# A convolution and two expert layers in one program: copy order in a bank's release, a shared bank for mixed halves, and a re-planned head

## The chip, the core and the metric

The kernel runs on one core of one Trainium2 chip. The core has five engines that run side by side, each through its own list of instructions in a fixed order: TensorE (PE) multiplies matrices into the eight PSUM banks, VectorE (DVE), ScalarE (ACT) and GpSimd (POOL) work elementwise, and SyncE (SP) issues DMAs. GpSimd has no access to PSUM here; everything it reads and writes is in SBUF. An engine whose next instruction waits for a semaphore holds up all that stands behind it. The metric is the device time of one execution, the median of several; smaller is better.

## The reference

Three layers follow each other on 2 batches of 4160 tokens with 192 features, all in float32 (the weights arrive as 64-bit floats and are narrowed on the chip):

```python
# 1: a causal convolution of 7 taps, weights per token and head
w = softmax(weight_gen)                       # 8 heads x 7 taps
out = einsum('bshk,bskhg->bshg', w, x_unf)    # x_unf: 7 shifted copies of x
# 2: a mix with the token before, then a gated expert
xk = mu_k * x + (1 - mu_k) * x_prev;  xr = mu_r * x + (1 - mu_r) * x_prev
v = relu(xk @ w_k) ** 2 @ w_v;  x = sigmoid(xr @ w_r) * v        # d_ff = 1024
# 3: a second expert with a convolution of 3 taps over tokens
h = relu(x @ w_in);  c = sum_k conv_w[k] * h[shifted by k - 1]
out = (h * sigmoid(c)) @ w_out
```

## The kernel before

The sequence is cut into ten tiles of 256, 248, seven times 472, and 352 tokens. Features lie on partitions, tokens on columns. Each float32 product is made of a high and a low part (fp32r), so one chunk of 128 hidden units costs five matmuls going in and five coming out.

For each tile, GpSimd computes layer 1 token group by token group (`attention`): one multiplication of a 128x1344 piece by the softmax weights, two folding additions, one addition into `tok`. TensorE transposes `tok` into a bank of the pair `pa` (`mixing`, `flip`), ScalarE and VectorE make the two mixed halves (k = 0 for `xk`, k = 1 for `xr`), which are split into high (`hi`) and low (`lo`) parts; for the 64 remaining features four DMAs place them in `xB`. There are three such mixings per tile, u = 0, 2, 1. In the first tile the two mixed halves stood in the PSUM banks `am` and `ar`, which later hold the accumulated sums of `moe1`.

`moe1` runs eight chunks fi per batch: matmuls into `pa`, relu, square and a rounded copy on ScalarE, the remainder on VectorE, five matmuls into `am` (128 rows) and `ar` (64 rows and a shared 64-row part). `mix_out` empties the two banks after each batch: VectorE multiplies them by the gates (d1 for `ar`, d0 for `am`), ScalarE copies the rounded high parts into `x2` (a1 from `ar`, in two copies of 128 and 64 rows; a0 from `am`), VectorE writes the low parts (d3 from `ar`, d2 from `am`). Until these are done the next batch's first sums cannot be written. `moe2` is layer 3: eight chunks through the banks `pc`, summed in `bm` and `br`.

In the head, before and while the first tile runs, the weights are narrowed (`prepare`, `narrow`: one ScalarE instruction, then five on VectorE, through the banks `bm`, `br`, `pc`), split, and the softmax weights are computed (`softmax`: reduction, subtraction, exp, reduction, reciprocal, multiplication). ScalarE holds one function table at a time; going from Sigmoid to Exp or back is an ACT_TABLE_LOAD.

The order of each engine's list is written by a planner, `Program.schedule`. Every operation has a due time (`at(t, ...)`) and an assumed duration (`cost`); the planner plays the engines forward, takes on each engine the ready operation with the earliest due time, and emits the instructions in the order of their planned starts. So a changed assumed duration or due time moves instructions on all engines. In it a PSUM bank is one region whatever part is touched. `cost` took a VectorE reduction to go at 960 elements per microsecond, and it looked at the tensors other than the output when it asked whether a source lies in PSUM; for an in-place operation that list was empty.

Of the kernel before, what the change touches and what calls it, by code (L numbers as in the profile page):

```python
# [35 lines left out]
class Program:  # L36
# [37 lines left out]
    def cost(self, eng, method, out, ins, pointer):  # L74

        n = self.count(out)
        src = [self.space(x) for x in ins]
        if method == "dma_start":
            return 0.6, 0.0
        if eng == "PE":  # L80
            busy = max(n * 0.00045 + 0.002, 0.109)
            return busy, busy + 0.24
        if eng == "ACT":
            near = bool(src) and src[0] == "PSUM"
            p = 0.1 if pointer else 0.0
            return (0.06 if near else 0.09) + p + n / 1200, (0.2 if near else 0.24) + p + n / 1200
        if eng == "DVE":
            if method == "tensor_reduce":
                n = self.count(ins[0])
            if method == "reciprocal":  # L90
                return 0.07 + n / 160, 0.2 + n / 160
            if method in ("tensor_scalar", "tensor_copy", "memset") and "PSUM" not in src:
                return 0.07 + n / 1920, 0.2 + n / 1920
            stt = method == "scalar_tensor_tensor"
            return (0.13 if stt else 0.07) + n / 960, (0.26 if stt else 0.2) + n / 960
        if eng == "POOL":
            busy = 0.1 + (n / 455 if method == "tensor_tensor" else n / 270)
            return busy, busy + 0.12
        return 0.6, 0.6

    def schedule(self):
        n = len(self.ops)
        succ, left, ready, dur, late, moved = [[] for _ in range(n)], [0] * n, [0.0] * n, [0.0] * n, [0.0] * n, [0.0] * n
        shares = [False] * n
        log = {}
        for i, (eng, method, a, k, _, hold) in enumerate(self.ops):
            ready[i] = hold
            aps = [x for x in [*a, *k.values()] if hasattr(x, "tensor") and hasattr(x, "ap")]
            out = k["out"] if "out" in k else aps[0]
            ins = [x for x in aps if x is not out]  # L110
            dur[i], late[i] = self.cost(eng, method, out, ins, any(x is not None and x in ("scale",) and hasattr(k[x], "tensor") for x in k))
            if method == "dma_start":
                moved[i] = self.count(out) * out.ap[0][1] * 4 / 240e3 if self.space(out) != "DRAM" else self.count(ins[0]) * ins[0].ap[0][1] * 4 / 240e3

            src = [self.space(x) for x in ins if self.count(x) > 1]
            shares[i] = eng == "POOL" or eng == "DVE" and (
                src == ["SBUF", "SBUF"] or method in ("tensor_scalar", "tensor_copy") and self.space(out) == "SBUF" and src == ["SBUF"])
            before = set()
            for x, write in [(x, False) for x in ins] + [(out, True)]:
                name, p0, p1, f0, f1 = self.region(x)  # L120
                seen = log.setdefault(name, [])
                keep = []
                for e in seen:
                    j, w, q0, q1, g0, g1 = e
                    if (w or write) and p0 < q1 and q0 < p1 and f0 < g1 and g0 < f1:
                        before.add(j)
                        if write and p0 <= q0 and q1 <= p1 and f0 <= g0 and g1 <= f1 and j != i:
                            continue
                    keep.append(e)
                keep.append((i, write, p0, p1, f0, f1))  # L130
                log[name] = keep
            before.discard(i)
            left[i] = len(before)
            for j in before:
                succ[j].append(i)
        free = dict.fromkeys(self.real, 0.0)
        port, table = 0.0, None
        wires = dict.fromkeys(self.real, 0.0)
        open_ = {e: [] for e in self.real}
        for i in range(n):  # L140
            if not left[i]:
                open_[self.ops[i][0]].append(i)
        start = [0.0] * n
        for _ in range(n):
            t, eng = min((max(free[e], min(ready[i] for i in w)), e) for e, w in open_.items() if w)
            i = min((i for i in open_[eng] if ready[i] <= t), key=lambda i: (self.ops[i][4], i))
            open_[eng].remove(i)
            if shares[i]:
                t = max(t, port)
                port = t + dur[i]  # L150
            turn = 0.0
            if eng == "ACT" and self.ops[i][1] == "activation" and self.ops[i][2][2] in (ACTF.Exp, ACTF.Sigmoid):
                turn = 0.0 if self.ops[i][2][2] == table else 1.3
                table = self.ops[i][2][2]
            start[i] = t
            free[eng] = t = t + turn
            free[eng] += dur[i]
            end = t + late[i]
            if self.ops[i][1] == "dma_start":
                wires[eng] = max(wires[eng], t + dur[i] + 0.6) + moved[i]  # L160
                end = wires[eng] + 0.8
            for j in succ[i]:
                ready[j] = max(ready[j], t + dur[i] if eng == "PE" == self.ops[j][0] else end)
                left[j] -= 1
                if not left[j]:
                    open_[self.ops[j][0]].append(j)
        for i in sorted(range(n), key=lambda i: (start[i], i)):
            eng, method, a, k = self.ops[i][:4]
            getattr(self.real[eng], method)(*a, **k)  # L169
# [14 lines left out]
def conv_moe_kernel(ctx: ExitStack, tc: tile.TileContext, xp, wg_first, wg_rest, mus, w_k, w_v, w_r, w_in, conv_w, w_out, out):  # L184
    nc = tc.nc
    prog = Program(nc)
    PE, ACT, DVE, POOL, SP = (prog.engine(e) for e in ("PE", "ACT", "DVE", "POOL", "SP"))
# [59 lines left out]
    att_r = ring("att", 2, [128, NMAX])  # L247
# [35 lines left out]
    def at(t, fn, hold=0.0):  # L283
        plan.append((t, len(plan), fn, hold))
# [169 lines left out]
    def mixing(i, u, t, dt_):  # L454
        N, P, e = SIZES[i], PART[i], EXTRA[i]
        c = 1 if u == 2 else 0
# [11 lines left out]
        def shifted(fn):  # L468
            a = att_r()[:, :N]
            if e:  # L470
                fn(a, st["q"][:, e - 1:e + N - 1])
            else:
                POOL.memset(a[:, 0:1], 0.0)
                fn(a[:, 1:N], st["q"][:, 0:N - 1])
            return a

# [2 lines left out]
            DVE.tensor_tensor(a, a, st["p"], op=ALU.subtract)  # L479

        def m1(k):
            st[k] = (am_r, ar_r)[k]() if i == 0 else mk_r()
            col = 2 * k + c
            own = slice(col, col + 1)
            if i < 2:
                a = shifted(lambda y, x: ACT.activation(y, x, ACTF.Copy, scale=onemu[:, own]))
                DVE.scalar_tensor_tensor(out=st[k][:, :N], in0=st["p"], scalar=mu[:, own], in1=a, op0=ALU.mult, op1=ALU.add)
            else:
                DVE.scalar_tensor_tensor(out=st[k][:, :N], in0=st["d"], scalar=onemu[:, own],
                                         in1=st["p"], op0=ALU.mult, op1=ALU.add)  # L490
# [120 lines left out]
    def mix_out(i, b, t):  # L611
        N = SIZES[i]
        X = x2[b]
        c = slice(2, N + 2)
        m, r = am_r.tiles[0], ar_r.tiles[0]

        def d0():
            DVE.tensor_tensor(m[:, :N], r_t[0][:, :N], m[:, :N], op=ALU.mult)

        def d1():  # L620
            DVE.tensor_tensor(r[:, :N], r_t[1][:, :N], r[:, :N], op=ALU.mult)

        def a0():
            ACT.copy(X[:, 0, c], m[:, :N])

        def a1():
            ACT.copy(X[:, 2, c], r[:, :N])
            ACT.copy(X[0:64, 3, c], r[0:64, :N])

        def d2():  # L630
            DVE.tensor_tensor(X[:, 1, c], m[:, :N], f(X[:, 0, c]), op=ALU.subtract)

        def d3():
            DVE.tensor_tensor(X[64:128, 3, c], r[0:64, :N], f(X[0:64, 2, c]), op=ALU.subtract)

        at(t, d1)
        at(t + 0.14, d0)
        at(t + 0.15, a1)
        at(t + 0.3, a0)
        at(t + 0.4, d3)  # L640
        at(t + 0.5, d2)
# [94 lines left out]
    def identity():  # L736
        POOL.memset(ident, 0.0)
        POOL.affine_select(out=ident, in_=ident, compare_op=ALU.not_equal, fill=1.0, base=0,
                           pattern=[[-1, 128]], channel_multiplier=1)

    at(-101, identity)
    at(-100.5, consts)
    softmax_load(0, wg_first, -100)
    softmax(0, 0, slots[0], DVE, (-95, -94.9, -94.8, -94.7, -94.6, -94.5), am_r.tiles[0])
    attention(0, 0, -99.9, -90, 0.1, POOL)
    attention(0, 1, -99.6, -83.7, 0.1, POOL)
    softmax_load(1, wg_rest[:, :slots[1] * KH], -99.5)
    softmax(1, 0, slots[1], POOL, (-82.6, -82.5, -82.4, -82.35, -82.3, -82.25), ar_r.tiles[0])
    prepare((-99.75, -99.7, -99.4), [(-82, chunk_rem(w_k, wkB, True)), (-81, chunk_in(w_k, wkA, 0)),
                                     (-0.5, chunk_out(w_v, wv, 0)), (0.4, chunk_out(w_v, wv, 1)), (1.0, chunk_in(w_k, wkA, 1)),  # L750
                                     (1.4, chunk_out(w_v, wv, 2)), (2.4, chunk_out(w_v, wv, 3)), (3.4, chunk_r()),
# [99 lines left out]
```

## Time and profile before

| | us |
|---|---|
| median of 3 runs | 779.31 |
| lowest, highest run | 778.96, 781.27 |
| profiled execution | 780.29 |
| its span from first to last instruction | 778.5 |
| outside the span (780.29 less 778.5) | 1.79 |

Busy times over the whole span are PE 694.1 us (89%), ACT 665.5 us (85%), DVE 630.8 us (81%) and POOL 506.6 us (65%). Such shares average over three unlike stretches: the head up to about 160 us, in which weights are narrowed and the first tiles pass; the long middle; and the drain of the last tile from about 740 us. The profile gives the TensorE clock that was granted, as a share of full speed: its mean over the span is 0.974. A row of a timeline reads: start, duration, engine, line, operation, tensor written, tensors read, count, and in brackets how long the engine sat idle before it and what ended that. Almost all instructions carry L169, the planner's emitting line, so they are told apart by their tensors.

### The profile page before, as it was taken

The page shows a single profiled execution, that of the slowest core. Times are in us where ns is not written, and L with a number is a line of the kernel's source. Part 1 is how long each engine was busy: PE and PEld are TensorE (multiplying, and loading weights), DVE is VectorE, ACT ScalarE, POOL GpSimd, SP SyncE. Part 2 cuts the span into 40 slices and gives each one's busy share as a digit, 9 for nine tenths or more (in the row PEclk, how much of TensorE's full clock was granted, in tenths as well). Part 3 has the DMA queues.
Part 4 walks back from the last instruction along what each step waited for, and adds up shares of the span by engine and source line. Part 5 has one row for each costly group of instructions (what it writes and reads, how often), then busy time and mean ns, then how long its engine had stood idle before and what let it go on. Part 6 is the DMA issues. An engine that isn't in the chain of part 4 may idle for free.

```text
span 778.5 us, 10782 instructions
## 1 busy us (share of the span) xinstructions
PE 694.1 (89%) x3505; PEld 606.3 (78%) x3505; DVE 630.8 (81%) x1137; ACT 665.5 (85%) x1441; POOL 506.6 (65%) x368
## 2 busy tenths in 40 slices
PE   0065776999999999999999999999999999999985
PEld 0054676898888888888888888888888888888974
DVE  6997977886878787878787888788788878788886
ACT  2466797998989898989998989898989899999985
POOL 6998888899999999999999798565702010110000
PEclk9996886999999999999999999999999999999999
DMA  7685010130130112111221120120002000200000
GB/s 224 197 269 180 4 52 11 58 105 11 62 101 18 53 70 51 70 51 52 69 70 51 39 78 20 45 63 7 20 0 70 1 19 1 57 0 19 19 2 28
DMA packets 19240, 45.09 MB, mean 58 GB/s; under 512 B 3056, under 2 KB 14704, under 8 KB 19056
## 3 DMA queue, kind: packets, MB, share of 16 engines
q1 hardware_dynamic: 19184, 44.41, 18.9%
q8 instruction: 27, 0.44, 0.2%
q14 instruction: 29, 0.24, 0.1%
HBM read 27.40 MB, written 6.39 MB: 43 GB/s over the span
## 4 chain that ended last, share of the span: by engine, by line
PE 68%; ACT 14%; DVE 14%; issue 2%; DMA 1%; SPq 0%; ACTq 0%; DVEq 0%
PE pa L169 21%; PE pc L169 16%; PE am L169 10%; PE bm L169 9%; PE ar L169 7%; PE br L169 6%; DVE pc L169 4%; ACT pa L169 2%; DVE stage L169 2%; ACT pc L169 2%; ACT h L169 2%; ACT g L169 2%; ACT L169 1%; DVE bm L169 1%; DVE s L169 1%
## 5 line engine op out<-in xcount | busy, mean ns | idle before, releaser
L169 DVE SCALAR_TENSOR_TENSOR pc<-h,cw,pc 128x472 f32<-128x472 f32 (+3 forms) x312 | 203.7, 653 | 34.9 <-ACT pc L169 31.9
L169 POOL TENSOR_TENSOR prod<-rows,sw 128x1344 f32<-128x1344 f32 x70 | 216.1, 3087 | 11.0 <-DMA rows<-in_x_dram 6.0
L169 ACT ACTIVATE pa<-pa 128x472 f32<-128x472 f32 (+3 forms) x324 | 162.7, 504 | 37.9 <-PE pa L169 33.8
L169 POOL TENSOR_TENSOR prod<-prod 128x576 f32<-128x576 f32 (+1 forms) x140 | 171.2, 1223 | 8.6
L169 PE MATMUL am<-s,wv 128*128 128x472 f32 (+3 forms) x480 | 146.9, 366 | 7.5 <-ACT s L169 6.0
L169 PE MATMUL bm<-g,wo 128*128 128x472 f32 (+3 forms) x465 | 144.5, 361 | 9.6 <-ACT g L169 9.0
L169 DVE TENSOR_TENSOR pc<-h,pc 128x472 f32<-128x472 f32 (+3 forms) x156 | 92.6, 594 | 54.4 <-ACT pc L169 53.0
L169 PE MATMUL pa<-xA,wkA 128*128 128x472 f32 (+3 forms) x480 | 124.4, 363 | 7.5 <-DVE s L169 3.5
L169 PE MATMUL pc<-x,wiA 128*128 128x474 f32 (+3 forms) x468 | 118.6, 361 | 3.2 <-DVE g L169 3.2
L169 POOL TENSOR_TENSOR xA<-mk,xA 128x472 fp32r<-128x472 f32 (+2 forms) x36 | 40.5, 1130 | 122.1 <-ACT xA L169 95.8
L169 PE MATMUL ar<-s,wv 128*128 128x472 f32 (+3 forms) x320 | 112.0, 362 | 5.0 <-DVE x L169 3.3
L169 PE MATMUL br<-g,wo 128*128 128x472 f32 (+3 forms) x310 | 109.4, 356 | 0.0
L169 DVE TENSOR_TENSOR s<-pa,s 128x472 fp32r<-128x472 f32 (+3 forms) x162 | 94.9, 586 | 16.0 <-ACT s L169 15.0
L169 PEld LDWEIGHTS am<-s,wv 128*128 128x128 f32 x480 | 88.7, 196 | 22.4 <-ACT s L169 11.2
L169 DVE TENSOR_TENSOR g<-pc,g 128x472 fp32r<-128x472 f32 (+3 forms) x153 | 90.4, 591 | 16.4 <-ACT g L169 14.9
L169 PEld LDWEIGHTS bm<-g,wo 128*128 128x128 f32 x465 | 86.5, 192 | 21.1 <-ACT g L169 11.5
L169 PEld LDWEIGHTS pa<-xA,wkA 128*128 128x128 f32 x480 | 86.4, 196 | 19.8 <-DVE s L169 6.3
L169 ACT ACTIVATE pc<-h,cw 128x472 f32<-128x472 f32 (+3 forms) x156 | 97.5, 625 | 1.6
L169 PEld LDWEIGHTS pc<-x,wiA 128*128 128x128 f32 x468 | 84.3, 194 | 14.0 <-DVE g L169 4.5
L169 ACT ACTIVATE h<-pc 128x474 f32<-128x474 f32 (+3 forms) x156 | 82.5, 529 | 9.6 <-PE pc L169 7.5
L169 PE MATMUL pa<-xB,wkB 128*128 128x472 f32 (+3 forms) x320 | 89.0, 359 | 1.1 <-DMA xB<-mk 1.1
L169 PE MATMUL pc<-x,wiB 128*128 128x474 f32 (+3 forms) x312 | 87.4, 359 | 0.0
(121 smaller groups left out, 1086.9 us busy)
## 6 DMA issues: line engine op xcount, KB each, us to landing
rows<-in_x_dram SPq DMA_DIRECT2D x14, 960.0 KB, 4.5
xB<-rm SPq DMA_DIRECT2D x28, 118.0 KB, 2.3
xB<-mk SPq DMA_DIRECT2D x28, 118.0 KB, 2.3
out_dram<-om SPq DMA_DIRECT2D x14, 236.0 KB, 2.0
rows<-in_x_dram SPq DMA_DIRECT2D x4, 768.0 KB, 6.6
rows<-in_x_dram SPq DMA_DIRECT2D x2, 864.0 KB, 4.3
out_dram<-ob SPq DMA_DIRECT2D x14, 118.0 KB, 2.2
stage<-in_moe_w_v_dram SPq DMA_DIRECT2D x4, 384.0 KB, 3.8
```

What stands on the lines that cost most here:

```text
L169: getattr(self.real[eng], method)(*a, **k)
```

## The change

Five edits. `cost` now takes a VectorE reduction at 515 elements per microsecond, and an in-place operand counts as a source. In the first tile both mixed halves stand in one bank: columns 0 to 255 and 256 to 511 of `ar`; the softmax of the second tile's weights uses `am` in place of `ar`, and its due times are earlier. The column of zeros in front of a first token is set once in each `att` buffer by VectorE, where GpSimd set it before each of the six uses. And of the two copies out of `ar`, the 64-row one is issued first.

```diff
-                n = self.count(ins[0])
+                return 0.05 + self.count(ins[0]) / 515, 0.15 + self.count(ins[0]) / 515
...
-            ins = [x for x in aps if x is not out]
+            ins = [x for x in [*a[0 if "out" in k else 1:], *(v for key, v in k.items() if key != "out")]
+                   if hasattr(x, "tensor") and hasattr(x, "ap")]
...
-                POOL.memset(a[:, 0:1], 0.0)
                 fn(a[:, 1:N], st["q"][:, 0:N - 1])
...
-            st[k] = (am_r, ar_r)[k]() if i == 0 else mk_r()
+            st[k] = ar_r.tiles[0][:, 256 * k:256 * k + 256] if i == 0 else mk_r()
...
         def a1():
+            ACT.copy(X[0:64, 3, c], r[0:64, :N])
             ACT.copy(X[:, 2, c], r[:, :N])
-            ACT.copy(X[0:64, 3, c], r[0:64, :N])
...
+    def before_first():
+        for a in att_r.tiles:
+            DVE.memset(a[:, 0:1], 0.0)
+
     at(-101, identity)
+    at(-100.9, before_first)
...
-    softmax(1, 0, slots[1], POOL, (-82.6, -82.5, -82.4, -82.35, -82.3, -82.25), ar_r.tiles[0])
+    softmax(1, 0, slots[1], POOL, (-83.85, -83.65, -83.64, -83.63, -83.62, -83.55), am_r.tiles[0])
```

No instruction of the computation is added or dropped but the memsets (six of GpSimd become two of VectorE) and the table loads, of which ScalarE's list has 14 before and 10 after. The rest is order. Three places show it.

VectorE, where the first batch leaves the banks `am` and `ar`. `x_0` is the `x2` buffer of batch 0, `bm`, `br`, `pc`, `stage`, `wiA`, `wo` belong to the narrowing of weights. Before:

```order
L169 TENSOR_TENSOR am<-r_97,am 128x256
L169 TENSOR_TENSOR ar<-r_98,ar 128x256
L169 TENSOR_SCALAR bm<-bm 128x512
L169 TENSOR_TENSOR s_99<-pa_111,s_99 128x256
L169 SCALAR_TENSOR_TENSOR bm<-stage,bm 128x512
L169 SCALAR_TENSOR_TENSOR mk_83<-pa_112,mu,att_81 128x248
L169 TENSOR_SCALAR pc_113<-bm 128x512
L169 TENSOR_SCALAR br<-br 128x384
L169 SCALAR_TENSOR_TENSOR stage<-stage,pc_113 128x512
L169 SCALAR_TENSOR_TENSOR br<-stage,br 128x384
L169 TENSOR_TENSOR bm<-bm,stage 128x512
L169 TENSOR_SCALAR pc_114<-br 128x384
```

The next row of that list is d3, `x_0_73<-ar`, and d2 stands three rows behind it. After:

```order
L170 TENSOR_TENSOR am<-r_97,am 128x256
L170 TENSOR_TENSOR ar<-r_98,ar 128x256
L170 TENSOR_TENSOR wo<-bm,wo 128x2x128
L170 TENSOR_SCALAR br<-br 128x24
L170 TENSOR_TENSOR x_0_73<-am,x_0_73 128x256
L170 SCALAR_TENSOR_TENSOR br<-stage,br 128x24
L170 TENSOR_TENSOR wo<-bm,wo 128x2x64
L170 TENSOR_SCALAR pc_114<-br 128x24
L170 TENSOR_TENSOR s_99<-pa_111,s_99 128x256
L170 SCALAR_TENSOR_TENSOR stage<-stage,pc_114 128x24
L170 TENSOR_TENSOR x_0_73<-ar,x_0_73 64x256
```

Between the gate products and d3 stood ten instructions, eight of them 384 or 512 columns wide; now d2 stands there with seven others, four of 24 columns.

ScalarE, where the softmax of the later tiles needs exp (`sw<-sw`) between the sigmoids of layer 3 (`pc<-pc`). Before:

```order
L169 ACT_TABLE_LOAD
L169 ACTIVATE sw<-sw 128x448
L169 ACT_TABLE_LOAD
L169 ACTIVATE pc_114<-pc_114 128x256
L169 ACTIVATE h_103<-pc_113 128x258
L169 ACTIVATE pa_112<-pa_112 128x248
L169 ACTIVATE pc_113<-h_103,cw 128x256
L169 CAST g_102<-pc_114 128x256
L169 CAST s_100<-pa_112 128x248
L169 ACT_TABLE_LOAD
L169 ACTIVATE sw<-sw 128x448
L169 ACT_TABLE_LOAD
```

After, the last group of exps:

```order
L170 ACT_TABLE_LOAD
L170 ACTIVATE sw<-sw 128x448
L170 CAST g_101<-pc_113 128x256
L170 ACTIVATE pc_114<-h_104,cw 128x256
L170 ACTIVATE sw<-sw 128x448 x2
L170 ACTIVATE sw<-sw 128x336
L170 ACTIVATE h_103<-pc_113 128x258
L170 ACTIVATE pa_111<-pa_111 128x248
L170 ACT_TABLE_LOAD
```

Seven exps stood in six groups, each with a load on both sides; they now stand in four groups.

TensorE, in the second batch of the first tile (`xA_88`, `pa`, `am`, `ar` are `moe1`; `pc<-x_0` is `moe2` of the first batch). Before, `moe2` begins inside the matmuls of the fourth chunk of eight:

```order
L169 MATMUL am<-s_100,wv 128x256
L169 MATMUL ar<-s_100,wv 128x256
L169 MATMUL pa_111<-xA_88,wkA 128x256 x3
L169 MATMUL pc_113<-x_0_73,wiA 128x258 x3
L169 MATMUL pc_113<-x_0_73,wiB 128x258 x2
L169 MATMUL pa_111<-xB_92,wkB 128x256 x2
```

After, it begins between the second batch's last sums:

```order
L170 MATMUL pa_111<-xA_88,wkA 128x256 x3
L170 MATMUL pa_111<-xB_92,wkB 128x256 x2
L170 MATMUL am<-s_99,wv 128x256
L170 MATMUL ar<-s_99,wv 128x256
L170 MATMUL pc_113<-x_0_73,wiA 128x258 x3
L170 MATMUL pc_113<-x_0_73,wiB 128x258 x2
L170 MATMUL am<-s_100,wv 128x256 x2
```

Before, six chunks of `moe2` began ahead of the second batch's last sums; now one does, and the other five stand among the second tile's chunks.

## Rows read from the trace of the kernel before

**Rows 1.** Busy us of PE, PEld, DVE, ACT, POOL by stretch; clock, DMA share, GB/s.

```profile
40.00:160.00 120.00, 88.17 (x535) 80.16 (x536) 99.11 (x224) 98.06 (x256) 106.05 (x82) 0.84 0.29 92
160.00:740.00 580.00, 575.79 (x2814) 500.98 (x2814) 469.85 (x789) 527.43 (x1095) 369.49 (x256) 1.00 0.14 43
740.00:778.50 38.50, 27.84 (x154) 24.19 (x152) 29.89 (x60) 26.87 (x64) 0.00 (x0) 0.95 0.05 15
```

**Rows 2.** Waits of TensorE up to 160 us: waiter, releaser, total, times, longest.

```profile
PE bm L169 <- ACT g L169: 8.4, 4, 2.5
...
PE ar L169 <- DVE x L169: 3.3, 1, 3.3
```

**Rows 3.** Timeline of GpSimd before the first tile's last tokens.

```profile
28.68 0.66 POOL L169 TENSOR_TENSOR sw<-sw,smz 128x224 f32<-128x224 f32 x1 [0.92 <-ACT wv L169]
...
36.60 0.59 POOL L169 TENSOR_TENSOR tok<-prod 128x192 f32<-128x192 f32 x1
```

**Rows 4.** Timeline of VectorE, ScalarE and TensorE at the first matmuls.

```profile
38.78 0.56 DVE L169 SCALAR_TENSOR_TENSOR br<-stage,br 128x384 uint32<-128x384 uint32 x1
...
39.64 0.48 DVE L169 SCALAR_TENSOR_TENSOR ar<-pa,mu,att 128x256 f32<-128x256 f32 x1
...
39.76 0.37 ACT L169 CAST rm<-am 128x256 fp32r<-128x256 f32 x1 [1.10 <-DVE am L169]
...
40.27 0.98 PE L169 MATMUL pa<-xA,wkA 128*128 128x256 f32 x3 [2.33 <-ACT rm L169]
```

**Rows 5.** Timeline of VectorE at the release of the first batch's banks.

```profile
65.56 0.43 DVE L169 TENSOR_TENSOR am<-r,am 128x256 f32<-128x256 f32 x1 [1.30 <-PE am L169]
65.90 0.42 DVE L169 TENSOR_TENSOR ar<-r,ar 128x256 f32<-128x256 f32 x1
...
71.91 0.42 DVE L169 TENSOR_TENSOR x<-ar,x 64x256 fp32r<-64x256 f32 x1
...
73.43 0.42 DVE L169 TENSOR_TENSOR x<-am,x 128x256 fp32r<-128x256 f32 x1
```

**Rows 6.** Timeline of TensorE at the same release.

```profile
72.48 0.98 PE L169 MATMUL ar<-s,wv 128*128 128x256 f32 x3 [3.28 <-DVE x L169]
```

**Rows 7.** Timeline of ScalarE around one exp between two sigmoids.

```profile
88.97 1.28 ACT L169 ACT_TABLE_LOAD   x1
90.26 0.58 ACT L169 ACTIVATE sw<-sw 128x448 f32<-128x448 f32 x1
90.86 1.28 ACT L169 ACT_TABLE_LOAD   x1
...
95.46 0.37 ACT L169 CAST g<-pc 128x256 fp32r<-128x256 f32 x1 [2.00 <-DVE pc L169]
```

**Rows 8.** The chain that ended last: first and last load between 90 and 130.

```profile
96.85 1.28 ACT L169
...
123.51 1.28 ACT L169
```

**Rows 9.** Timeline of VectorE: the reductions in a row.

```profile
89.51 5.16 DVE L169 TENSOR_REDUCE stage<-sw 128x64 f32<-128x448 f32 x6
```

**Rows 10.** ScalarE by form: count, busy us, mean ns, idle before.

```profile
L169 ACT ACT_TABLE_LOAD x14 | 18.0, 1283 | 3.8 <-DMA sw<-in_first_dram 3.6
...
L169 ACT CAST g<-pc 128x256 fp32r<-128x256 f32 x16 | 6.1, 379 | 3.7 <-DVE pc L169 3.5
```

**Rows 11.** Busy times of shorter stretches of the head, columns as in Rows 1.

```profile
45.00:60.00 15.00, 11.69 (x69) 10.24 (x68) 13.07 (x27) 11.72 (x34) 14.30 (x10) 1.00 0.95 281
60.00:80.00 20.00, 12.17 (x56) 10.43 (x57) 16.10 (x41) 12.39 (x37) 17.89 (x17) 0.62 0.50 158
...
100.00:130.00 30.00, 19.31 (x115) 17.66 (x113) 22.90 (x50) 28.68 (x66) 25.47 (x21) 0.82 0.10 37
```

**Rows 12.** Timeline: last token group of the fourth tile, and a transpose of it.

```profile
200.00 0.61 POOL L169 TENSOR_TENSOR tok<-prod 128x192 f32<-128x192 f32 x1
...
212.07 0.60 PE L169 MATMUL pa<-ident,tok 128*128 128x128 f32 x4
```

## The prediction

> **What bounds the kernel now.** I read the busy times by stretch first, since the page's shares mix unlike ones. From 160 to 740 us TensorE is busy for 575.79 of 580 us at full clock [rows 1]: the middle is bound by TensorE, and what order and copies do there can win at most the remaining 4.2 us. The matmuls are the same in both kernels, so whatever the head gives or takes reaches the end almost one to one. In the head, from 40 to 160 us, TensorE is busy for 88.17 of 120 us at a mean clock of 0.84, while POOL has 106.05, DVE 99.11 and ACT 98.06 [rows 1]. No engine is full there; the head is a chain that passes from one to another, so I read it by its waits and its timeline.
>
> Three places stand out. The first real matmul starts at 40.27, after the last token group of the first tile at 36.60 [rows 3, 4]. From 69.2 to 72.48 TensorE waits for VectorE to empty the bank `ar` [rows 6]. And between 88.97 and 130 ACT is nearly full, 28.68 of the 30 us from 100 on [rows 11], with twelve table loads in this stretch; TensorE's largest wait in the head after the token groups is for ACT's `g`, 8.4 us in four waits [rows 2].
>
> The profiled execution took 780.29 us, a span of 778.5 and 1.79 around it. It lies 0.98 above the median of 779.31. I make the sum on 780.29 and take off 0.98 at the end.
>
> **The start of the first tile.** POOL waits 0.92 us for a reciprocal before it can multiply the second tile's weights [rows 3]. In the new order that multiplication stands ahead of the second token group, and the 448-column one behind the next large product; both are still ahead of the last group, so POOL's work up to it is the same, and only the wait can go, with 0.14 us of memsets. On VectorE the two mixing instructions of the second mixing (39.64 is the second) stand behind the 384-column `br` step of 38.78 [rows 4]; now they stand two such steps earlier with one between them. The steps start 0.4 to 0.5 apart, so this is worth about 0.4. I take 0.92 + 0.4 = 1.3; bounds 0 (the reciprocal is late again) and 1.8 (two steps). The two zeros that VectorE sets lie ahead of all its work and cost nothing; if they delayed it, it would be by their own length, of the order of POOL's 0.14.
>
> **One bank for two halves.** Before, the first rounding on ACT starts at 39.76 while VectorE still writes the other half, from 39.64 for 0.48, into another bank [rows 4]. With both halves in one bank the dependencies are kept by bank, so ACT waits for the second half, 0.4 us later, and VectorE's subtraction waits for both roundings. That stands in three mixings, but the first one's result lies ready long before the matmul of 40.27, and the third one's is needed behind the DMAs of the second. I charge one: +0.4; bounds 0 and 2.6 (three times 0.48 + 0.37 from [rows 4]).
>
> The Trainium skill, "PSUM — Partial Sum Buffer", section "PSUM bank collisions raise a hardware error", speaks against this edit: it says that ACT and VectorE must not touch one bank on the same partitions at one time, whatever the columns, and have to be kept apart by semaphores. The overlap that the row at 39.76 shows is between two banks and so agrees with it; by that rule the overlap cannot survive the change, and the sum by it is the one with the 0.4 in it.
>
> **The release of the first batch's banks.** VectorE multiplies `ar` by its gate at 65.90, but writes the last low part only at 71.91 to 72.33 [rows 5]; ten instructions stand between, eight of them weight narrowing of 384 or 512 columns. TensorE waits 3.28 us for it [rows 6]. The new order leaves d2 and seven others between, four of them of 24 columns, and d2 moves up from 73.43. Eight wide steps of some 0.5 less four narrow ones takes off more than the wait is long, so all 3.28 should go: -3.3; bounds 0 (ACT's two copies become late in VectorE's place) and 6.4 (from 65.90 to 72.33, if the clock recovers with it). The swapped copies within it change nothing that TensorE sees: both must be read before d3 in either order, and steady-state waits are inside the 4.2 us above.
>
> **Table loads.** A load takes 1283 ns, fourteen times [rows 10]; ten are left. Four loads are 5.1 us of ACT. Not all of ACT's time there is on the path: of the twelve loads from 88.97 to 130, eight are pieces of the chain that ended last, the first at 96.85 and the last at 123.51 [rows 8]. I take 5.1 x 8/12 = 3.4; bounds 0 (others become late) and 5.1.
>
> The row shows the load of 88.97 over at 90.25 and the exp starting at 90.26, then the next load right behind the exp [rows 7]: a switch costs 1.28 us and no more. The Trainium skill, "ScalarE: Activation LUTs", section "What ACT_TABLE_LOAD costs", gives some 1.28 us for the load and 1.38 for a drain, 2.66 per switch. By the page four switches would be 10.6 us, and this term 7.1; the rows show no drain, and the row decides.
>
> **The reductions.** VectorE runs six in a row, 5.16 us from 89.51 [rows 9], since the planner took one to cost half of what it does; ACT then waits 2.00 us at 95.46 for the product behind them [rows 7]. In the new order they stand in ones and twos. A pair can still hold a product up, so I take half: -1.0; bounds 0 and 2.0.
>
> **`moe2` behind the second batch.** Five chunks of `moe2` leave the second batch's `moe1`. Alone, `moe1` passes through ACT and VectorE with only two banks, and ACT idles: in the first batch 15 - 11.72 = 3.3 us from 45 to 60 [rows 11]. Against that stands the idle time of the mixed stretch, 20 - 12.39 = 7.6 from 60 to 80 [rows 11], which has the stall above in it. I charge +1.0, below the 3.3 because narrowing work lies in that stretch too; bounds -2 and +3.3.
>
> **The drain.** TensorE idles 38.5 - 27.84 = 10.7 us from 740 on [rows 1], and the order changes there a little. I take 0, with 1 us either way.
>
> **The sum.** -1.3 + 0.4 - 3.3 - 3.4 - 1.0 + 1.0 = -7.6, so 780.29 - 7.6 = 772.7 for an execution like the profiled one, and 771.7 for the median.
>
> **Rivals.** (a) *The work that moves back is too much for ACT.* If the second batch's `moe1` doesn't become shorter without `moe2` in it, because narrowing sets its pace, five chunks with four ACT instructions each, 20 x 0.379 = 7.6 us [rows 10], arrive in a stretch where ACT is already full [rows 11]. With the start and the loads gained and no gain at the release, that is 779.31 + 7.6 - 1.3 - 3.4 = 782.2, slower. It decides from the point where the five chunks cost more than the 4.7 us gained. For it speaks VectorE's 13.07 of 15 us busy from 45 to 60 [rows 11]; against it, that the second batch's weights for layer 2 are all narrowed before.
>
> (b) *POOL sets the pace.* It is the busiest engine of the head with 106.05 of 120 us [rows 1], and its token groups come only 0.92 earlier. Then TensorE meets their waits earlier and gains only that: 778.4. Against it: the fourth tile's last group ends at 200.61 and its transpose comes at 212.07 [rows 12], so TensorE can move forward by 11.5 us there before it meets POOL.
>
> (c) *The clock stays up.* From 60 to 80 us TensorE is busy for 12.17 us at a mean clock of 0.62, from 100 to 130 for 19.31 at 0.82 [rows 11]. At full clock this work would be 12.17 x 0.38 + 19.31 x 0.18 = 8.1 us shorter. If the shorter stalls keep the clock at its 2.4 GHz level for two thirds of it, another 5.5 us go: 766.2. Against it: where TensorE waits for ACT, a faster matmul only waits longer.
>
> (d) *The edits don't reach the chip as planned.* The planner's times still differ from the chip's, waits shift, and the gains and losses cancel: 779.3.
>
> **How the numbers follow.** Chances: the forecast 0.60, (a) 0.10, (b) 0.09, (c) 0.17, (d) 0.04. About 0.3%, 2.3 us, is what a measurement of this kernel tells from no change. The forecast's cases end at about 777 and (c) is faster too: faster 0.78. (b), (d) lie within 0.3%: same 0.13. (a): slower 0.09. The range: all bounds on the good side without the clock give 1.8 + 6.4 + 5.1 + 2.0 + 2, 17 us, which POOL's 11.5 and 0.92 cut to about 12.4; with less than all of it, the low end is 765.5, where (c) is just inside. The high end, with the start and a part of the loads alone, is 777.5. About 2 in 10 lie outside, mostly above.
>
> **What would show it.** Right: the first matmul near 39; no wait of TensorE for `x` near 70, and the first sums of the second batch before 69; ten loads; no run of six reductions; the stretch in which TensorE stays above 98% busy begins some 8 us earlier, with the middle as long as before. Wrong: TensorE waiting for `tok` after the first tile (b), ACT full and TensorE waiting for `g` over a longer stretch (a), or a new wait where `moe1` of the second batch runs alone.

## The result, and the profile after

The changed kernel takes 771.25 us (median of 4 runs, 770.81 to 771.41), against 779.33 us (median of 4) for the kernel before, measured beside it: a ratio of 0.989, with a 95% interval from 0.9873 to 0.9908. The profiled execution took 771.41 us with a span of 769.6. The forecast was 771.7. The time came out as forecast, but for the wrong reasons: about half of it goes with an edit that the prediction priced at nothing, and the two largest terms of its sum win nothing when they are taken alone in the kernel before.

The busy times of the changed kernel by stretch (columns as in [rows 1] and [rows 11]):

```profile
40.00:160.00 120.00, 92.15 (x570) 82.54 (x570) 102.89 (x232) 96.42 (x263) 107.73 (x81) 0.87 0.33 98
160.00:740.00 580.00, 577.30 (x2825) 503.01 (x2823) 472.65 (x793) 528.96 (x1097) 366.45 (x254) 1.00 0.14 42
740.00:769.60 29.60, 21.73 (x107) 16.74 (x107) 23.57 (x49) 20.63 (x49) 0.00 (x0) 0.95 0.06 19
45.00:60.00 15.00, 12.32 (x77) 11.15 (x77) 12.33 (x25) 12.82 (x35) 13.02 (x9) 1.00 0.97 296
60.00:80.00 20.00, 15.11 (x84) 13.52 (x84) 14.67 (x36) 12.82 (x40) 17.87 (x17) 0.74 0.55 170
100.00:130.00 30.00, 20.39 (x131) 19.08 (x130) 25.67 (x53) 25.19 (x60) 27.00 (x21) 0.83 0.01 5
```

From 160 to 740 us TensorE now idles for 2.7 us instead of 4.2. From 60 to 80 us it does 15.11 us of work where it did 12.17. ScalarE is no longer full from 100 to 130 us, 25.19 for 28.68, but VectorE has 25.67 for 22.90 there: the crowd has moved, it has not gone.

TensorE's waits up to 160 us in the changed kernel (columns as in [rows 2]): the wait for VectorE's `x` is gone, that for ScalarE's `g` is smaller, and one for ScalarE's `s` has grown from 4.3 to 7.7 (the last row is the one before the change).

```profile
PE am L170 <- ACT s L170: 7.7, 6, 3.6
PE bm L170 <- ACT g L170: 6.1, 6, 2.6
...
PE pa L170 <- DVE ar L170: 4.8, 2, 2.6
```
```profile
PE am L169 <- ACT s L169: 4.3, 5, 1.4
```

The places of [rows 3] to [rows 6] in the changed kernel, GpSimd and TensorE at the start, then VectorE and TensorE at the release of the first batch's banks:

```profile
32.10 1.13 POOL L170 TENSOR_TENSOR sw<-sw,smz 128x448 f32<-128x448 f32 x1
...
35.75 0.59 POOL L170 TENSOR_TENSOR tok<-prod 128x192 f32<-128x192 f32 x1
```
```profile
39.34 0.98 PE L170 MATMUL pa<-xA,wkA 128*128 128x256 f32 x3 [2.25 <-DVE ar L170]
42.89 0.98 PE L170 MATMUL pa<-xA,wkA 128*128 128x256 f32 x3 [2.58 <-DVE ar L170]
...
65.24 0.77 PE L170 MATMUL am<-s,wv 128*128 128x256 f32 x2 [1.73 <-DVE br L170]
...
67.31 0.41 PE L170 MATMUL ar<-s,wv 128*128 128x256 f32 x1
```
```profile
63.77 0.42 DVE L170 TENSOR_TENSOR ar<-r,ar 128x256 f32<-128x256 f32 x1
...
64.66 0.43 DVE L170 TENSOR_TENSOR x<-am,x 128x256 fp32r<-128x256 f32 x1
...
65.93 0.42 DVE L170 TENSOR_TENSOR x<-ar,x 64x256 fp32r<-64x256 f32 x1
```

The last token group of the first tile is 0.85 earlier, and so is the first matmul (0.93). The subtraction on `ar` follows its gate product by 2.16 instead of 6.01 us, and the first sums into `ar` start at 67.31 without a wait, 5.17 us earlier. Something of the release is left: the first sums into `am` (65.24) wait 1.73 us. The row names `br`, but VectorE's low part from `am` ends only just before, at 65.09. There are ten table loads, and the run of six reductions is gone.

**A clock for both traces.** One instruction stands once in each batch: VectorE's product of `ar` with its gate. Its start in the seventh batch marks the end of the head, in the eighteenth the end of the middle. From these rows of all the profiled executions:

```
                       seventh  eighteenth  between    span
before                  270.73    684.30     413.57    778.5
after                   265.31    676.55     411.24    769.6
e1 costs alone          263.78    680.68     416.90    773.8
e2 edits alone          263.83    675.11     411.28    768.2
e3 old start            263.96    675.81     411.85    768.9
e4 copies back          264.58    681.36     416.78    774.5
e5 copies alone         270.42    681.50     411.08    774.6
e6 copies in place      264.65    676.04     411.39    769.1
e7 four more loads      270.17    681.41     411.24    774.5
e8 release alone        272.76    686.32     413.56    780.5
e9 exps together        271.10    682.48     411.38    775.6
e10 edits, exps tog.    263.32    673.91     410.59    767.0
e11 two banks           267.89    679.29     411.40    772.4
e12 four loads less     270.28    683.95     413.67    778.1
```

Before to after: 5.4 us of the span are won in the head, 2.3 in the middle, 1.2 behind it; together 8.9. The head of one execution is known only to some 2 us: the same mark in the first batch stands at 65.90, 67.10, 67.27 and 65.10 in before, e5, e8 and e12, whose programs are alike up to there, and the profiled executions of e1 and e4 are the fastest of their 12, 1.5 and 2.2 us below the medians. The middle is not so loose: it takes only three lengths, near 411, 413.6 and 416.8.

### The profile page after: what moved, and what is told of

Same layout as the page of the kernel before. It is cut to its first block, busy times and chain, and to the rows that moved or that the text cites. A ratio compares the mean times of both kernels' runs of the same rounds, so it can differ in the third digit from the quotient of the medians.

```text
span 769.6 us, 10775 instructions
## 1 busy us (share of the span) xinstructions
PE 694.2 (90%) x3505; PEld 603.9 (78%) x3505; DVE 629.8 (82%) x1139; ACT 659.3 (86%) x1437; POOL 505.8 (66%) x362
## 4 chain that ended last, share of the span: by engine, by line
PE 76%; ACT 13%; DVE 4%; DMA 2%; issue 2%; POOL 1%; SPq 0%; ACTq 0%; DVEq 0%
PE pa L170 24%; PE pc L170 17%; PE am L170 11%; PE bm L170 10%; PE ar L170 7%; PE br L170 6%; ACT pc L170 2%; ACT pa L170 2%; ACT h L170 1%; ACT L170 1%; POOL prod L170 1%; ACT g L170 1%; ACT s L170 1%; DVE pc L170 1%; DMA stage<-in_moe_w_k_dram 1%
## 5 line engine op out<-in xcount | busy, mean ns | idle before, releaser
L170 PE MATMUL pc<-x,wiA 128*128 128x474 f32 (+3 forms) x468 | 120.7, 362 | 1.5 <-DVE stage L170 1.1
```

## Experiments: which edit

**e1, the two planner prices alone** (the kernel before with these lines of the change):

```diff
-                n = self.count(ins[0])
+                return 0.05 + self.count(ins[0]) / 515, 0.15 + self.count(ins[0]) / 515
...
-            ins = [x for x in aps if x is not out]
+            ins = [x for x in [*a[0 if "out" in k else 1:], *(v for key, v in k.items() if key != "out")]
+                   if hasattr(x, "tensor") and hasattr(x, "ap")]
```

> The kernel before with the two corrected planner prices alone (reductions at 515 elements per us, operands written in place counted as sources); start, banks and copies as before. The order it gives has 8 table loads, d3 and d2 right behind the two gate products, moe1 of the second batch nearly alone, reductions in ones and twos. Theory (prices by place: release 3.3, loads 0.85 each, reductions 1, moe2 behind the second batch +1): 779.3 - 3.3 - 5.1 - 1 + 1 = 771, 769 to 773; first matmul still near 40.3; no wait of TensorE for x near 70. Rival 1 (what reaches the end comes from the new start and the shared bank; the orders behind it are worth little): 777 to 779. Rival 2 (all edits add up, each with its share): about 773 to 775.

Measured: 777.02 us (12 runs) against 779.95, ratio 0.9964 (0.9954 to 0.9975). Theory and rival 2 both miss; the time lies at the lower end of rival 1's range. But the table shows a head 7 us shorter than that of before (some 5 by the median of e1), and a middle that is 3.3 us longer.

**e2, the other edits alone** (the changed kernel with those two prices put back).

> The changed kernel with both planner prices as before: new start, one bank for the first tile's halves, zeros by VectorE, 64-row copy first. Its order too has 8 table loads and d2, d3 within four instructions of the gate products, but three reductions in a row and moe2 beginning earlier. Theory (prices by place, whichever edit brings the place about): 779.3 - 0.9 - 3.3 - 5.1 = 770, 768 to 773. Rival (the corrected prices themselves carry the gain, since the planner's times fit the chip only with them): 776 to 779.

Measured: 769.6 us (4 runs), ratio 0.9866 (0.985 to 0.9882). As the theory said; the corrected prices don't carry the gain.

**e3, the old start** (the changed kernel with GpSimd's zeros, two banks for the halves and the old due times and bank of the second softmax).

> The changed kernel with the old start: zeros by GpSimd, two banks for the halves, the second tile's softmax in the other bank with the old due times. 8 table loads, release as short as in the changed kernel. Theory: the start costs 0.9 to 1.3, two loads less give 1.7 back: 771.3 + 0.9 - 1.7 = 770.5, 769 to 772.5; first matmul near 40.2. Rival (the start is what the gain came from): 774 to 778.

Measured: 771.13 us (4 runs), ratio 0.9887 (0.9871 to 0.9903). The start is not where the gain comes from. e3 is e1 with the copies swapped, and nothing else: 5.9 us between the medians.

**e4, the copies back:**

```diff
-            ACT.copy(X[0:64, 3, c], r[0:64, :N])
             ACT.copy(X[:, 2, c], r[:, :N])
+            ACT.copy(X[0:64, 3, c], r[0:64, :N])
```

> The changed kernel with the 128-row copy ahead of the 64-row one again; every other instruction stands where it stood. Theory of the prediction (the swap changes nothing that TensorE sees): 771.3 within 0.5. Rival (in the middle TensorE's 1.7 us of waits for ACT's x behind the bank release, seven of them, are there before and gone after, and the ACT's 64-row copy waits 3.2 us in all for VectorE before and 0.0 after): 772.5 to 773.5, with these waits back in the trace.

Measured: 778.47 us (12 runs), ratio 0.9979 (0.9969 to 0.999). Putting two copies back costs nearly the whole gain, far more than even the rival said. One thing in the expectation was wrong: only the head keeps its order. From the third tile on the planner answers with another order of VectorE's two subtractions and of TensorE's sums. One batch of the middle in e4, ScalarE, VectorE and TensorE:

```profile
417.27 0.60 ACT L170 CAST x<-ar 128x472 fp32r<-128x472 f32 x1
...
418.12 0.64 DVE L170 TENSOR_TENSOR x<-ar,x 64x472 fp32r<-64x472 f32 x1
418.56 0.59 PE L170 MATMUL pa<-xB,wkB 128*128 128x472 f32 x2
...
418.79 0.55 ACT L170 CAST x<-ar 64x472 fp32r<-64x472 f32 x1 [0.46 <-DVE x L170]
...
419.39 0.70 PE L170 MATMUL ar<-s,wv 128*128 128x472 f32 x2 [0.23 <-ACT x L170]
...
419.93 0.80 PE L170 MATMUL pc<-x,wiA 128*128 128x474 f32 x3
```

The same place in the changed kernel:

```profile
415.95 0.57 ACT L170 CAST x<-ar 64x472 fp32r<-64x472 f32 x1
...
416.84 0.58 ACT L170 CAST x<-ar 128x472 fp32r<-128x472 f32 x1
...
417.24 0.59 PE L170 MATMUL pa<-xB,wkB 128*128 128x472 f32 x2
...
417.67 0.80 PE L170 MATMUL am<-s,wv 128*128 128x472 f32 x3
417.90 0.64 DVE L170 TENSOR_TENSOR x<-ar,x 64x472 fp32r<-64x472 f32 x1
418.31 0.59 PE L170 MATMUL pc<-x,wiA 128*128 128x474 f32 x2
```

In e4 VectorE's subtraction reads the bank `ar` between ScalarE's two copies of it. The 64-row copy does not start until that read is over, though neither writes the bank, and TensorE, which is to write new sums into it, waits for the copy. The Trainium skill, "PSUM — Partial Sum Buffer", section "PSUM bank collisions raise a hardware error", says that two engines must be kept apart on the same partitions of one bank, two readers too; the 0.46 us, a wait for a semaphore of VectorE by the profile, agree. The named wait is 0.23, but the stop costs more: from 418.56 to 419.93 TensorE issues four matmuls in 1.37 us, where five take 1.07 in the changed kernel (417.24 to 418.31), so four 0.86. A stop costs 0.5 us. The named wait counts from the end of the matmul ahead (419.15), but one of 0.38 us is followed by the next after 0.21, so this one could have started at 418.99. And its weights, which are else loaded while the matmul ahead still runs (PEld), are loaded only now:

```profile
418.35 0.41 PEld L170 LDWEIGHTS pa<-xB,wkB 128*128 128x128 f32 x2
419.39 0.30 PEld L170 LDWEIGHTS ar<-s,wv 128*128 128x128 f32 x2 [0.64 <-ACT x L170]
```

These are TensorE's waits for this copy from 160 us on, in e4, in e1 and in the kernel before; in the changed kernel there is none:

```profile
PE ar L170 <- ACT x L170: 2.8, 12, 0.2
```
```profile
PE ar L170 <- ACT x L170: 2.9, 12, 0.2
```
```profile
PE ar L169 <- ACT x L169: 1.7, 7, 0.2
```

The kernel before has them in every other batch, six of the seven between the two marks. That gives the three lengths of the middle: no stop (411), six (413.6), one in each batch (416.8; eleven stops, 5.5 us), so 0.4 to 0.5 us a stop. By the medians e4 is 7.2 us behind the changed kernel; where the rest goes, its profiled execution does not show.

**e5, the copies alone** (the kernel before with the 64-row copy first).

> The kernel before with the 64-row copy first, and nothing else; the order of the head is the old one, behind it the planner answers with other orders. Theory S (in the kernel before, in every other batch, the 64-row copy waits for VectorE's read of the same bank and TensorE then stops; a stop has a named wait of 0.23 but takes 0.5 of the issue, 0.83 + 0.54 for four matmuls that else take 0.87): seven stops go, 780 - 3.5 = 776.5, 775.5 to 777.5, no wait of TensorE for x in the middle, the head as before. Rival L (the swap is worth the whole 7 us that taking it back cost): 772 to 774. Rival 0 (the prediction's: nothing): 779.5 to 780.5.

Measured: 775.39 us (6 runs) against 780.06, ratio 0.9946 (0.993 to 0.9961). Theory S holds, at the edge of its range: the ratio gives 4.2 us (3.0 to 5.5) for 3.5, about half of the whole change. In the trace the stops are gone and the middle is 2.5 shorter; the seventh mark is 0.3 earlier, and the part behind the eighteenth 1.1 shorter. That last part is not the stops: the kernel before has none there, and e1 and e4, with the old copies, are as short behind that mark (93.1 us, for 94.2 before). It is another order.

**e6, the copies exchanged in place** (the changed kernel with all orders kept but this one):

```diff
+        for (_, _, part), i in self.tag.items():
+            if part == "a1":
+                start[i], start[i + 1] = start[i + 1], start[i]
         for i in sorted(range(n), key=lambda i: (start[i], i)):
```

> The changed kernel with every engine's order kept and the two copies of a bank exchanged in their places on ScalarE: the 128-row copy first, but VectorE's subtraction still behind both. Theory S (what costs is the 64-row copy that waits for VectorE's read of the bank, not which copy is first): no stop, 771.3 within 0.7. Rival (the order of the copies itself costs, whoever reads between them): 774 to 778.

Measured: 771.54 us (4 runs), ratio 0.989 (0.9876 to 0.9904), the same as the changed kernel. So it is not the order of the copies that counts, but whether VectorE's read falls between them. The edit works because the subtraction reads what the 128-row copy writes (`X[0:64, 2, c]`) and nothing of the 64-row one: with the 128-row copy second, it must stand behind both. No run moved the subtraction alone; that the stops are its doing rests on the rows above, on e6, and on the lengths of the middle, which go by the number of stops.

## Experiments: what the terms of the head are worth

**e7, four more loads** (the changed kernel, two exps followed by a sigmoid of one column):

```diff
+            if i in [exps[e] for e in (3, 4)]:
+                self.real["ACT"].activation(self.spare, self.spare, ACTF.Sigmoid)
```

> The changed kernel with every order kept and two sigmoids of one column put between exps of the last softmax, which bring the table loads from 10 to 14 as before the change, all between 105 and 115 us. Price in the prediction: 0.85 a load, 3.4 for four, so 774.7 (773.5 to 776 with the two small sigmoids). Rival (ScalarE's loads there are hidden by waits that stay, or the clock gives it back): 771 to 772. Rival (all of it is on the path): 776.5 and more.

Measured: 776.41 us (6 runs), ratio 0.9961 (0.9946 to 0.9976). That is 5.2 us for four loads and two small sigmoids of 0.2: in the changed kernel nearly all of a load is on the path, 1.2 to 1.3 us and not 0.85. TensorE's longest wait for `s` grows from 3.6 to 7.16 us:

```profile
122.13 0.79 PE L171 MATMUL am<-s,wv 128*128 128x248 f32 x2 [7.16 <-ACT s L171]
```

**e12, four loads less in the kernel before** (orders kept, three exps moved up behind the exp ahead of them):

```diff
+        for first, second in ((2, 3), (4, 5), (5, 6)):
+            start[exps[second]] = start[exps[first]] + 0.001
```

> The kernel before with every order kept but for three exps of the last softmax, which are moved up behind the exp ahead of them: 10 table loads for 14, as many as in the changed kernel. Theory (a load in this stretch is 1.3 on the path, as four more cost in the changed kernel): 780.1 - 5.2 = 774.9, 774 to 776; then the loads and the swapped copies (4.7) carry the whole change. The prediction's price, 0.85 a load: 776.7. Rival (as in the kernel with the exps held together: a load that goes gives its time to another wait): 778 to 780.5.

Measured: 780.21 us (12 runs) against 779.9, ratio 1.0 (0.9985 to 1.0015). The rival holds: the term that the prediction put at 3.4 us is worth nothing by itself. The trace says where it went. VectorE and GpSimd of e12 at the first load that is missing, then at the last, and the first place in the kernel before:

```profile
114.92 2.42 DVE L172 TENSOR_SCALAR stage<-stage 128x64 f32<-128x64 f32 x1
...
121.93 0.19 DVE L172 TENSOR_SCALAR stage<-stage 128x64 f32<-128x64 f32 x1
...
126.08 1.71 DVE L172 TENSOR_SCALAR stage<-stage 128x64 f32<-128x64 f32 x1
```
```profile
114.22 3.06 POOL L172 TENSOR_TENSOR prod<-rows,sw 128x1344 f32<-128x1344 f32 x1
...
124.68 3.06 POOL L172 TENSOR_TENSOR prod<-rows,sw 128x1344 f32<-128x1344 f32 x1
```
```profile
114.87 3.06 POOL L169 TENSOR_TENSOR prod<-rows,sw 128x1344 f32<-128x1344 f32 x1
...
116.39 1.59 DVE L169 TENSOR_SCALAR stage<-stage 128x64 f32<-128x64 f32 x1
```

An addition over 64 columns takes VectorE 0.19 us when GpSimd is not in a product, and 2.42 and 1.71 when it is: it ends at 117.34 and 127.79, 0.06 and 0.05 after GpSimd's product (117.28, 127.74). In the kernel before the same addition starts 1.47 later, at 116.39, and takes 1.59, to 117.98, again just behind GpSimd's product of 114.87 to 117.93. This execution of e12 is 0.65 us ahead from the start (second mark at 103.95 for 104.60), and behind the two additions it still is, no more: what ScalarE gave, VectorE spent waiting for GpSimd. The Trainium skill, "SBUF — State Buffer", section "SBUF: two separate sides", says that the two engines share a pair of ports as an exclusive lock, held for a whole instruction, and that a VectorE instruction in a two-port mode blocks against it. The rows agree; in which mode the addition runs they do not show. The planner has such a lock too (`shares`), but with the old list of sources it saw none in an addition done in place, and so left this one out of it; the corrected list puts it in. That alone does not end these waits: in e1 and e3, which have the corrected list, one such addition still takes 2.46 and 2.55 us.

**e9 and e10, the exps held together** (a time before which the planner may not start them, 108 in the changed kernel, 104 in e2):

```diff
-            at(t, fn)
+            at(t, fn, 108 if j == 3 and fn is s3 else 0.0)
```

> The changed kernel with the seven exps of the last softmax held back in the planner until they can run together: 4 table loads for 10, the rest of the head in the order that the planner then finds. Theory (a load in the stretch from 95 to 125 us is 1.3 on the path, as four more loads cost 5.1): six less give 771.3 - 7.7 = 763.6, 763 to 766 with what the held exps delay. Rival (past the first loads something else sets the pace there, VectorE with 18.6 of 20 us busy or GpSimd with 18.7): 768 to 771. Rival (the weights of the fourth tile come too late and TensorE waits for tok): 771 and more, with a wait for tok behind 160 us.

> The kernel of the edits alone (old planner prices, 769.6) with the exps held back in the same way: 4 table loads for 8. Theory (1.3 a load): 769.6 - 5.1 = 764.5, 763.5 to 766.5. Rival (VectorE or GpSimd sets the pace): 768 to 769.6. Rival (late weights): 770 and more.

Measured: e9 777.47 us (6 runs) against 780.28, ratio 0.9964 (0.9952 to 0.9976); e10 768.4 us (4 runs), ratio 0.9846 (0.9833 to 0.9859). Six loads less made the changed kernel 6 us slower, four less made e2 1.2 us faster by the medians, with intervals that overlap. So the theory fails in both. e10 lies in the range of its first rival, and e9 in that of the late weights, but there was no late token. The planner's order of the head is another one in both, so the loads are not the only difference. In e9 ScalarE begins the load ahead of the exps at 117.43 and is back at the sigmoids at 125.35, and VectorE's sums over them come late and in a row. TensorE meets both:

```profile
123.20 0.38 PE L170 MATMUL br<-g,wo 128*128 128x256 f32 x1 [3.03 <-DVE ob L170]
126.99 0.79 PE L170 MATMUL am<-s,wv 128*128 128x248 f32 x2 [2.72 <-ACT s L170]
...
140.64 0.79 PE L170 MATMUL bm<-g,wo 128*128 128x256 f32 x2 [2.92 <-ACT g L170]
```

From 120 to 140 us it is busy for 9.41 us at a granted clock of 0.62 (17.68 at 0.96 in the changed kernel). So fewer loads can cost more than they give where the exps are held for them. e10 is by its median the fastest kernel of this study.

**e8, the release alone** (the kernel before, orders kept, the two subtractions of the first batch moved up):

```diff
+        for d, a in (("d3", "a1"), ("d2", "a0")):
+            start[self.tag[0, 0, d]] = start[self.tag[0, 0, a]] + 0.001
```

> The kernel before with every order kept but for two instructions: VectorE's two low parts of the first batch are moved up, each right behind the copy that it needs, ahead of the weight narrowing. Price in the prediction: 3.3, so 780 - 3.3 = 776.7 (775.5 to 778), and no wait of TensorE for x near 70. Rival (the time comes back in the crowded stretch that follows, up to 130 us, where ScalarE is full): 779 to 780, with the wait at 70 gone but TensorE's waits for ScalarE up by as much.

Measured: 781.27 us (12 runs) against 780.06, ratio 1.0018 (1.0008 to 1.0029): nothing won, a little lost. The wait for `x` goes and another takes its place, for the mixing product behind the same weight narrowing. TensorE and VectorE of e8:

```profile
72.68 0.58 PE L171 MATMUL ar<-s,wv 128*128 128x256 f32 x1 [1.01 <-ACT s L171]
...
76.80 1.01 PE L171 MATMUL pa<-xA,wkA 128*128 128x256 f32 x3 [2.47 <-DVE mk L171]
```
```profile
68.88 0.42 DVE L171 TENSOR_TENSOR x<-ar,x 64x256 fp32r<-64x256 f32 x1
...
70.81 0.43 DVE L171 TENSOR_TENSOR x<-am,x 128x256 fp32r<-128x256 f32 x1
...
76.28 0.47 DVE L171 SCALAR_TENSOR_TENSOR mk<-pa,mu,att 128x248 f32<-128x248 f32 x1
```

The 3.28 us of [rows 6] covered a second wait. The changed kernel has no such wait at its 67.31; there the whole order of narrowing is another one, and `moe2`, which needs the narrowed weights, begins later.

**e11, two banks again** (the changed kernel, orders kept, the second half of each mixing in `am`; a table maps its operands when they are issued):

```diff
+            if i == 0 and k == 1:
+                prog.other[id(st["x", k])] = am_r.tiles[0][:, :N]
```

> The changed kernel with every order kept, the second half of each mixing of the first tile in another bank again, so that ScalarE's rounding and VectorE's writing of the two halves are no longer kept apart by the bank. Price of the shared bank in the prediction: 0.4, so 770.9 (770 to 771.5). Rival (TensorE's two waits for VectorE's ar at 39 and 42 us, 2.25 and 2.58 in the changed kernel, are there for the bank and reach the end): 768.5 to 769.5. Rival (hidden behind the DMAs of the second mixing): 771.3.

Measured: 771.83 us (5 runs, 769.82 to 774.24), ratio 0.9883 (0.9867 to 0.9899). Sharing the bank costs nothing that can be measured here; 0.4 is below what this tells. The rival with 2 us or more falls: the two waits of 39 and 43 us come to 4.1 together with two banks, for 4.8 with one.

## Why the prediction was right in its time and wrong in its parts

**The step that failed** is the sentence "The swapped copies within it change nothing that TensorE sees: both must be read before d3 in either order, and steady-state waits are inside the 4.2 us above." The swap is worth 4.2 us (e5; 3.0 to 5.5), about half of the change, and 2.5 of it are the stops of the middle. Two things were wrong. It is not so that both must be read first: with the old order the subtraction needs only the 128-row copy, and falls between the two copies in batches of the middle; the rows that I had read are of the head [rows 5], where it comes late. And a stop was counted at its named wait: seven waits of 0.23 are 1.7 us of the trace, but each takes 0.4 to 0.5 of time. That the sum still met the time is luck: it left this out, and it had 3.3 and 3.4 us in it that win nothing alone in the kernel before. Of the signs that it named, the middle "as long as before" did not come; it is 2.3 us shorter.

**The start** (-1.3): 0.93 at the first matmul, within its bounds; e3, which has the old one and another order behind it, is as fast as the changed kernel, so that it is not seen at the end.

**The shared bank** (+0.4): not distinguishable from nothing (e11).

**The release** (-3.3): the wait for `x` went as forecast, and the first sums into `ar` are 5.2 us earlier. But moving the two subtractions alone wins nothing (e8). What I priced was a wait, and a second one stood behind it; "what is late next" was the question that this step did not ask.

**Table loads** (-3.4): the number has no single value. Four loads cost 5.2 in the changed kernel (e7) and 0 in the kernel before (e12). That loads are pieces of the chain that ended last [rows 8] did not show what taking them out would give; GpSimd's products stood beside them, in rows that the chain does not name.

**Reductions and `moe2`** (-1.0 and +1.0): the run of six is gone and `moe2` begins at 83.92 instead of 78.24; neither was taken alone. **The drain** (0): 1.2 us shorter behind the eighteenth mark. The copies alone bring 1.1 of it (e5), but so do the two prices alone (e1), so it belongs to no one edit.

**What the head is worth**, then, is the largest part: 5.4 of the 8.9 us by the marks (4.4 by the ratios, 8.6 less 4.2 for the copies with all that goes with them). It belongs to no one edit. e1 and e2 have no edit in common, and both have a seventh mark 6.9 us ahead of before (some 5 for e1 by its median); e3 has it 6.8 ahead. By this the order of before was a poor one, and several changes to the planner's input lead away from it. Why the planner finds it with the old numbers, and how it divides among the narrowing that comes later, the reductions and the loads, stays open.

**The rivals.** (a) did not happen: ScalarE was less busy, and the waits for `g` fell. (b) was named for the wrong place: no token came late, but GpSimd held VectorE up in a stretch of the kernel before (e12). (c) can't be told from the order: the mean clock of the head rose from 0.84 to 0.87, where 60 to 80 us went from 0.62 to 0.74. (d) fell, though e8 and e12 are two cases of it.

## What to carry to other kernels

Price a wait of an engine that is otherwise full by the time from the instruction before to the one after, not by the wait that the profile names, and multiply it by the steps of the loop before calling it small: 0.23 us was 0.4 to 0.5, and in the loop it came to 2.5 us, with one in each batch to 5.5. A piece of the critical chain is worth what it lasts only if nothing stands behind it at nearly the same time; take it out alone, with every order kept, before summing such pieces. And where a planner orders the work, an edit is one more draw of an order: two sets of edits with nothing in common each gave a shorter head.

## What the runs showed of the hardware

- In these programs two readers of one PSUM bank, ScalarE and VectorE, run one behind the other: a copy waits 0.46 us for a subtraction that only reads the bank, over the fourteen 64-row copies of 472 columns 5.5 us in e4, 3.2 in the kernel before and 0.0 in the changed one. The profile gives a semaphore as the reason; no run leaves it out.

```profile
L170 ACT CAST x<-ar 64x472 fp32r<-64x472 f32 x14 | 7.7, 548 | 5.5 <-DVE x L170 5.5
```
```profile
L169 ACT CAST x<-ar 64x472 fp32r<-64x472 f32 x14 | 7.7, 549 | 3.2 <-DVE x L169 3.2
```
```profile
L170 ACT CAST x<-ar 64x472 fp32r<-64x472 f32 x14 | 7.9, 565 | 0.0
```

- A VectorE addition of 64 columns takes 0.19 us, or up to 2.42 in e12 when a GpSimd product of 3.06 us is running; it then ends 0.05 to 0.06 us behind the product. A stop of TensorE that the profile names as 0.23 us takes 0.5 of its issue.
- A VectorE reduction of 448 columns to 64, read with a stride, takes 0.94 to 1.05 us by itself, and one of 224 to 32 0.54 to 0.56; ten table loads still take 1283 ns each.
